# Fused block-sorted attention and maxout feed-forward on one core: zero blocks in front of item 0's scores and values, split last stores, and a new hand-written order

## The chip, the cores and the metric

The kernel runs on one core of one Trainium2 chip. The metric is the device time in microseconds (us) of one execution. The core has five instruction streams that run side by side and meet only at semaphores: TensorE (PE, with its weight loads shown as PEld), VectorE (DVE), ScalarE (ACT), GpSimd (POOL) and SyncE (SP). Each stream runs its own instructions strictly in the order in which they were issued.

## What is computed

```python
for _ in range(5):                       # sort_net: 4 items x 8 heads x 8 x 8
    P = np.exp(P - P.max(-1)); P = P / P.sum(-1); P = P / P.sum(-2)
k_sorted = einsum('bhij,bhjcd->bhicd', P, k_blocks)   # 8 blocks of 96 rows, 64 wide
v_sorted = einsum('bhij,bhjcd->bhicd', P, v_blocks)
scores = q_block @ k_sorted_block.T / 8               # each block against its own
attn = softmax(scores); x = attn @ v_sorted_block     # 3072 tokens x 512
g = maximum(x @ w1, x @ w2)                           # 512 -> 1024, twice
out = g @ w_out                                       # 1024 -> 512, float32
```

There are 4 items (the batch) of 768 tokens. Since `max(a, b) = relu(a - b) + b`, the kernel replaces w1 by w1 - w2, takes a relu, and adds `x @ (w2 @ w_out)` to the output. The output product itself is made by a Strassen-like scheme of seven products and a few sums.

## The kernel before

After a common start (the five normalisations, loads and first sorts) the whole rest is a list of short tokens, read from left to right by `token` (L917). The list is the order: each token issues its instructions on the engines at once, and every engine then runs its own share in that order. A final letter names the engine that empties PSUM (A is ScalarE, D is VectorE) or does the elementwise work (P is GpSimd). The first number is the item, mostly.

- `k`, `b`: sort a third of an item's keys (`sort_k`, L443) or a part of its values (L467 to L529) on TensorE, then cast them to SBUF. `q`: transposes of the queries. For items 0 and 1 TensorE makes them (L427); for items 2 and 3 the SP queue issues a DMA transpose (L417) from what `p` packed.
- `s b.u`: scores of unit u (`scores`, L533): eight matmuls, then one exponential on ScalarE (L551). `v b.u`: values of the same unit (`values`, L562): eight matmuls that need that exponential, then a reciprocal and a product on VectorE (L581, L587). `x b.t`: transposes of the result, on TensorE for item 0 (L608), as DMA transposes from the SP queue for the others (L600). x0.0 needs units 0 and 1, x0.1 units 2 and 3, x0.2 units 4 and 5, x0.3 units 6 and 7.
- `d`: w1 - w2 for a quarter of the columns. `T`: TensorE transposes of w2 (L633). `c`: the product w2 @ w_out (L652). `B`: the block diagonals of the later items' sorts (L319 to L337). `h`, or `ha` and `hb` for its halves: the first feed-forward product (L672) and its relu (L686, L688).
- `X`, `G`, `w`: sums for the Strassen-like product. `P i.n` and `U i.n`: its steps 0 to 6 (`Group.step`, L847; matmuls L800) for two tiles of 128 tokens and for one tile. Steps 5 and 6 each end in a store of the rows of one half of the tokens (L838 to L845), on the SP queue: 512 KB for P, 256 KB for U.
- `l`: loads, issued by GpSimd: `lk` keys, `lq` queries, `lv` and `lf` values. `y`: a small GpSimd copy that waits for the item's DMA transposes and so holds back what GpSimd issues after it. `t`: turns values on VectorE.

All PSUM results come from one ring of four buffers, taken in the order of the list (L63, L68). A token that needs a buffer waits until the result made four tiles earlier has been read. `keep_streaming` (L78) multiplies zeros into a PSUM tile that is written over afterwards. `scores` and `values` have an argument `n` for such zeros, and the list before never sets it:

```python
def scores(b, u, n=0):
    ...
    ps = ps_f32("s_ps")
    keep_streaming(ps, n)
```

Of the kernel before, what the change touches and what calls it, by code (L numbers as in the profile page):

```python
# [16 lines left out]
def kernel(  # L17
# [16 lines left out]
    nc = tc.nc  # L34
# [4 lines left out]
    B, H, S, D = q.shape  # L39
# [4 lines left out]
    DMODEL = H * D  # L44
# [9 lines left out]
    NW = DMODEL // 2  # L54
# [12 lines left out]
    def ps_f32(name):  # L67
        return psum.tile([128, 1024], FP32, tag="ps", name=name)  # L68
# [93 lines left out]
    def load_v(b, pieces=2, which=None, half=None):  # L162
        r0 = (b % 2 if half is None else half) * 64
        n = BLK * D // pieces
        for m in range(pieces) if which is None else [which]:
            nc.gpsimd.dma_start(  # L166
                out=v_raw[r0 : r0 + 64, m * n : (m + 1) * n],
                in_=v_src[b, :, m * n : (m + 1) * n],
            )
# [30 lines left out]
    def selections(b, eng=nc.gpsimd):  # L200
# [8 lines left out]
        if b == 0:  # L209
# [9 lines left out]
        out=one_j.rearrange("g (j x) -> g j x", x=130)[:, :, 0:128].rearrange(  # L219
            "g j (h w) -> g j h w", w=16  # L220
        )[:, :, :, 0:2],
        in_=ident[0:G, 0:8].to_broadcast([G, 8, 2, NB]).transpose([0, 3, 1, 2]),
# [548 lines left out]
    class Group:  # L771
# [63 lines left out]
                ins = nc.scalar.copy(out=out, in_=self.by_tile(self.bank(n)))  # L835
            return self.read(ins, n)

        def store(self, ch):  # L838
            tok0 = self.b * S + ch * TCH + self.tiles[0] * 128
            nc.sync.dma_start(  # L840
                out=out[tok0 : tok0 + len(self.tiles) * 128, :].rearrange(
                    "(t p) n -> p t n", p=128
                ),
                in_=self.o[ch],
            )  # L845

        def step(self, at, eng):  # L847
            a = self.by_tile(self.a) if at else None
            if at == 0:
                n = len(self.tiles)  # L850
                self.ps = ps_f32("out_ps")
                self.a = opool.tile([128, self.w], FP32, tag=f"a{n}", name="a", bufs=1)
                self.o = [
                    opool.tile([128, n, DMODEL], FP32, tag=f"o{n}", name="o", bufs=2)
                    for _ in range(2)
                ]
                self.product(0, "a11", "b11", True)
                self.first = self.copy(self.by_tile(self.a), 0, eng)
            elif at == 1:
                self.product(1, 2, 2, True)  # L860
                self.second = self.add(1, 0, 1, a, [self.first], eng)
            elif at == 2:
                self.product(0, "a12", "b21", False)
                self.copy(self.part(0, 0), 0, eng)
            elif at == 3:
                self.product(1, 1, 1, False)
                self.third = self.add(0, 1, 1, a, [self.first], eng)
            elif at == 4:
                self.product(0, 3, 3, True)
                self.fourth = self.add(1, 1, 0, self.part(0, 1), [self.third], eng)  # L870
            elif at == 5:
                self.product(1, 4, "b22", False)
                self.fifth = self.add(0, 1, 1, a, [self.first, self.fourth], eng)
                self.store(0)
            else:
                self.product(0, "a22", 4, False)
                self.add(
                    1, 0, 0, self.part(1, 0), [self.first, self.second, self.fifth], eng, True
                )
                self.store(1)  # L880

    first, second, both = slice(0, 64), slice(64, 128), slice(0, 128)
    keep_streaming(ps_f32("fill_ps"), 92 * 118, most=118)
# [8 lines left out]
    for c, n, m in [(2, 2, 0), (4, 3, 1)]:  # L892
        nc.gpsimd.tensor_copy(
            out=maskJ[:, c : c + n],
            in_=maskJ[:, m].to_broadcast([128, NB, n]).transpose([0, 2, 1]),
# [21 lines left out]
    def token(text):  # L917

        eng = text[-1] if text[-1].isalpha() else None
        body = text[:-1] if eng else text  # L920
        kind = body.rstrip("0123456789.")
        n = [int(x) for x in body[len(kind) :].split(".")]
        engine = {"P": nc.gpsimd, "D": nc.vector}.get(eng)
        if kind == "k":
            sort_k(*n, eng=eng)
        elif kind == "q":
            q_transposes(*n, eng)
        elif kind == "s":
            scores(*n)
        elif kind == "v":  # L930
            values(*n)
        elif kind == "x":
            x_transposes(*n, eng)
        elif kind == "t":
            turn_v(slice(0, 128), eng, n[1] * 24, n[1] * 24 + 24)
        elif kind == "b":
            {0: sort_v, 2: sort_v_pair, 3: sort_v_halved}[n[0]](*n, eng=eng)
        elif kind == "p":
            pair_q(*n, eng)
        elif kind == "y":  # L940
            nc.gpsimd.tensor_copy(
                out=landed.rearrange("p (c h n) -> p c h n", c=2, n=1),
                in_=xT[:, n[0] % 2, :, :, 0, 0:1],
            )
        elif kind == "lv":
            load_v(3, half=n[0])
        elif kind == "lk":
            load_k(n[0])
        elif kind == "lq":
            load_q(n[0])  # L950
        elif kind == "w":
            weight_sums(*n, engine)
        elif kind == "c":
            w_product(n[0], eng)
        elif kind == "X":
            x_sums(*n, engine)
        elif kind == "G":
            g_sums(*n, engine)
        elif kind == "h":
            moe_h(*n, eng=eng)  # L960
        elif kind == "ha":
            moe_h_products(*n, (0, 2))
        elif kind == "hb":
            moe_h(*n, eng, (1, 3))
        elif kind == "T":
            w2_transposes(n[0], eng)()
        elif kind == "d":
            w_difference(n[0], engine)
        elif kind == "B":
            block_diagonals([(0, 2), (0, 3), (1, 1), (1, 2), (1, 3)], 2)  # L970
        elif kind == "lf":
            load_v(1 + n[0] % 2, which=n[0] // 2)
        else:
            key = kind, n[0]
            if key not in groups:
                groups[key] = Group(n[0], (0, 1) if kind == "P" else (2,), n[0] > 0)
            groups[key].step(n[1], eng)

    groups = {}
    landed = const.tile([128, 4], BF16, tag="landed", name="landed")  # L980
    plan = [
        """
        d0P d1P k0.2D k0.1A b0.1D b0.2A b0.0A q0.0D b0.3A B0 q0.1D lk1 s0.4 s0.5 s0.0 v0.4 s0.7
        s0.6 v0.5 s0.3 v0.7 s0.1 v0.0 x0.2A v0.6 s0.2 v0.3 T0A v0.1 x0.3D T1D ha0.1.0 lq1 v0.2
        lf2 d3D ha0.1.1 lf3 x0.0D hb0.1.0A x0.1D hb0.1.1D w0.1D ha0.0.3 d2D ha0.1.3 hb0.1.3D
        G0.1.1D hb0.0.3A X0.3D ha0.1.2 ha0.0.1 hb0.0.1D hb0.1.2D G0.1.2D ha0.0.0 hb0.0.0A lf1
        lf0 G0.1.4D G0.0.1D X0.1D X0.2D w0.3D k1.1D k1.0A k1.2A c1D G0.1.3D c2D q1.0D q1.1A c0A
        s1.7 t1.3D s1.5 c3A G0.0.2D t1.2D G0.0.3D X0.4D s1.1 lq2 w0.2D s1.6 w1.1D s1.4 ha0.0.2
        t1.1D t1.0D hb0.0.2A s1.0 w1.2D P0.0D b2.2A G0.0.4D b2.0A w1.3D b2.1D P0.1D b2.6A b2.3A
        P0.2A b2.7D w1.4D b2.5A b2.4A p2.0A w0.4D P0.3D U0.0A v1.6 v1.7 x1.3 P0.4D U0.1D v1.4  # L990
        v1.5 U0.2A lk2 lk3 p2.1A x1.2 q2.0 P0.5D U0.3D v1.1 v1.0 lq3 P0.6D U0.4D k2.1D s1.2 s1.3
        U0.5D U0.6D x1.0 v1.2 q2.1 k2.0D k2.2A v1.3 h1.1.1A x1.1 X1.1D h1.1.2A s2.5 s2.1 h1.1.3A
        h1.1.0D G1.0.1D y1 s2.4 k3.0A k3.2A k3.1A lv1 h1.0.2A X1.2D v2.1 p3.0D G1.1.1D h1.0.1A
        v2.4 h1.0.0A s2.3 p3.1D G1.0.2D s2.6 q3.0 G1.1.2D h1.0.3A v2.5 G1.1.3D P1.0A G1.1.4D
        s2.0 s2.2 s2.7 X1.4D P1.1D q3.1 P1.2A X1.3D G1.0.3D lv0 v2.6 v2.7 P1.3D U1.0A x2.3
        G1.0.4D x2.2 v2.2 P1.4D U1.1D v2.3 t3.0D P1.5D P1.6D U1.2A v2.0 U1.3D U1.4D s3.3 x2.0
        x2.1 s3.0 t3.3D s3.6 t3.1D t3.2D U1.5D U1.6D h2.1.3D b3.2A X2.1D b3.3D h2.1.0A h2.1.1A
        X2.2D b3.0D b3.1A h2.0.1D s3.2 G2.1.1D s3.5 X2.3D G2.1.2D h2.1.2A v3.0 h2.0.3A X2.4D
        v3.3 v3.2 h2.0.0A G2.0.1D G2.0.2D h2.0.2A P2.0D G2.1.4D G2.0.4D G2.1.3D s3.1 s3.7 s3.4
        P2.1D v3.1 P2.2A U2.0D G2.0.3D x3.1 U2.1D v3.7 v3.6 P2.3D U2.2D v3.5 U2.3D v3.4 x3.3  # L1000
        x3.0 P2.4D U2.4D x3.2 P2.5D U2.5D U2.6D P2.6D h3.0.0D h3.1.3D h3.1.1D h3.0.1D X3.1D
        X3.3D h3.1.0D h3.1.2A G3.1.1D U3.0D G3.1.3D h3.0.3A h3.0.2A G3.1.2D P3.0A G3.0.1D
        G3.0.2D X3.2D G3.0.4D U3.1D P3.1D X3.4D U3.2A P3.2D U3.3D G3.1.4D G3.0.3D P3.3D P3.4D
        P3.5D U3.4D P3.6D U3.5D U3.6D
        """,
    ]
    for part in plan:
# [30 lines left out]
```

## Time and profile before

| quantity | value |
|---|---|
| three runs, median (lowest to highest) | 162.42 us (161.79 to 163.26) |
| the profiled execution, its own time | 162.45 us |
| span of its instructions | 160.7 us |
| mean granted clock of TensorE over the span | 0.985 |
| TensorE busy | 152.5 us, 95% |
| VectorE busy | 124.4 us, 77% |
| ScalarE busy | 77.0 us, 48% |
| GpSimd busy | 33.0 us, 21% |

A busy share is taken over the whole span, so it mixes stages that have different limits. "Granted clock" is the share of its full rate at which TensorE was allowed to run. A chain of waits lists what ended last, followed back from the last instruction. Times inside the profile count from the start of the span, and the execution's own time is 1.75 us longer than the span.

### The profile page before, as it was taken

Reading aid. Unit: us, or ns where it says so; the run is one execution under the profiler, and the core shown is the slowest. Engines: PE = TensorE matmul, PEld = TensorE weight load, DVE = VectorE, ACT = ScalarE, POOL = GpSimd, SP = SyncE. Lnnn points to the kernel's source line nnn. Section 1 sums busy time; section 2 is a strip of 40 time slices with the busy share of each in tenths; the row PEclk is TensorE's granted clock in tenths of the full one; section 3 lists DMA queues with packets and bytes.
Section 4 is the critical chain, followed back from the end, with each engine's and each line's share of the span. In section 5 each row is a group of like instructions: output and inputs, shape, how many; then the busy total and the mean of one; then the engine's idle time right before and its main releaser. Section 6 shows DMA issues by size and latency. Waiting matters only on the chain.

```text
span 160.7 us, 5090 instructions
## 1 busy us (share of the span) xinstructions
PE 152.5 (95%) x2224; PEld 117.6 (73%) x2224; DVE 124.4 (77%) x269; ACT 77.0 (48%) x98; POOL 33.0 (21%) x62
## 2 busy tenths in 40 slices
PE   7999899999999999999999999999999999999970
PEld 7938679666556889885767998766789985678850
DVE  4878887989996879993478798988788857975650
ACT  3587996224279994157878600576651000250000
POOL 7959998241230100000320000000000000000000
PEclk9999987999999999999999999999999999999998
DMA  3999999999999999699699983730100594000054
GB/s 38 205 205 198 182 189 205 210 205 214 220 201 204 211 173 158 131 367 126 133 164 197 165 165 131 234 135 0 35 18 0 115 250 177 0 4 0 0 209 185
DMA packets 30310, 23.93 MB, mean 149 GB/s; under 512 B 16784, under 2 KB 24976, under 8 KB 30288
## 3 DMA queue, kind: packets, MB, share of 16 engines
q0 software_dynamic: 11040, 13.37, 49.5%
q1 hardware_dynamic: 19248, 10.23, 26.5%
q8 instruction: 17, 0.28, 0.7%
q14 instruction: 5, 0.04, 0.1%
HBM read 26.75 MB, written 6.29 MB: 206 GB/s over the span
## 4 chain that ended last, share of the span: by engine, by line
PE 86%; DMA 5%; ACT 3%; POOL 2%; issue 1%; DVE 0%; POOLq 0%
PE out_ps L800 35%; PE h_ps L672 26%; DMA k_raw<-in_k_dram 5%; PE o_ps L570 5%; PE wc_ps L652 5%; PE k_ps L452 4%; PE s_ps L542 4%; ACT e L551 2%; PE tq_ps L427 2%; PE tw_ps L633 1%; PE v_ps L517 1%; PE v_ps L473 1%; PE tx_ps L608 1%; POOL v_raw L166 1%; PE v_ps L494 1%
## 5 line engine op out<-in xcount | busy, mean ns | idle before, releaser
L672 PE MATMUL h_ps<-xT,w_sb 128*128 128x384 bf16 x256 | 44.8, 326 | 0.1
L672 PEld LDWEIGHTS <-w_sb 128*128 128x128 bf16 x256 | 23.9, 98 | 14.7
L686 ACT ACTIVATE g<-h_ps 128x768 bf16<-128x768 f32 x20 | 16.3, 813 | 33.2 <-PE h_ps L672 33.2
L551 ACT ACTIVATE e<-s_ps 96x768 bf16<-96x768 f32 x32 | 23.8, 807 | 7.6 <-PE s_ps L542 7.5
L587 DVE TENSOR_TENSOR x<-o_ps,rs 96x512 bf16<-96x512 f32 x32 | 22.0, 687 | 1.1
L800 PEld LDWEIGHTS <-g 128*128 128x128 bf16 x192 | 18.4, 98 | 2.2
L826 DVE TENSOR_TENSOR o<-out_ps,a 128x512 f32<-128x512 f32 (+1 forms) x24 | 13.2, 554 | 4.3 <-PE out_ps L800 3.2
L688 DVE TENSOR_SCALAR g<-h_ps 128x768 bf16<-128x768 f32 x12 | 11.4, 955 | 6.3 <-PE h_ps L672 6.3
L800 PEld LDWEIGHTS <-sums_g 128*128 128x128 bf16 x144 | 13.8, 98 | 1.7
L800 PE MATMUL out_ps<-wo_sb,g 128*128 128x256 bf16 x96 | 13.1, 273 | 0.0
L570 PE MATMUL o_ps<-v_sb,e 96*128 96x65 bf16 x256 | 12.6, 197 | 0.2
L570 PEld LDWEIGHTS <-e 96*128 96x128 bf16 x256 | 11.2, 100 | 1.8 <-ACT e L551 0.5
L800 PE MATMUL out_ps<-w2T,sums_x 128*128 128x256 bf16 x72 | 11.8, 273 | 0.0
L826 DVE TENSOR_TENSOR o<-out_ps,o 128x512 f32<-128x512 f32 (+1 forms) x16 | 8.7, 553 | 3.5 <-PE out_ps L800 3.2
L109 ACT CAST v_sb<-v_ps 96x1024 bf16<-96x1024 f32 x11 | 10.6, 1013 | 1.5 <-PE v_ps L494 1.1
L542 PEld LDWEIGHTS <-kT 64*128 64x128 bf16 x256 | 6.3, 95 | 4.5 <-issue 3.3
L542 PE MATMUL s_ps<-qT,kT 64*128 64x96 bf16 x256 | 8.6, 206 | 1.0 <-DVE qT L111 0.5
L800 PEld LDWEIGHTS <-sums_x 128*128 128x128 bf16 x96 | 8.6, 97 | 1.1
L109 ACT CAST kT<-k_ps 128x1024 bf16<-128x1024 f32 x8 | 7.8, 1015 | 2.6 <-PE k_ps L452 2.6
L581 DVE RECIPROCAL rs<-o_ps 96x8 f32<-96x8 f32 x32 | 6.3, 198 | 3.2 <-PE o_ps L570 3.1
L157 POOL DMA_DIRECT2D k_raw<-in_k_dram x12 | 6.7, 564 | 8.3 <-DMA q_raw<-in_q_dram 3.8
L835 ACT COPY o<-out_ps 128x512 f32<-128x512 f32 (+1 forms) x6 | 2.9, 480 | 11.3 <-PE out_ps L800 11.3
(116 smaller groups left out, 243.5 us busy)
## 6 DMA issues: line engine op xcount, KB each, us to landing
out_dram<-o SPq DMA_DIRECT2D x8, 512.0 KB, 3.0
k_raw<-in_k_dram POOLq DMA_DIRECT2D x12, 256.0 KB, 11.9
v_raw<-in_v_dram POOLq DMA_DIRECT2D x8, 384.0 KB, 12.4
out_dram<-o SPq DMA_DIRECT2D x8, 256.0 KB, 3.0
w_sb<-in_moe_w_dram POOLq DMA_DIRECT2D x4, 256.0 KB, 6.1
w_sb<-in_moe_w_dram POOLq DMA_DIRECT2D x2, 512.0 KB, 9.4
wo_sb<-in_moe_w_out_dram POOLq DMA_DIRECT2D x2, 512.0 KB, 12.8
v_raw<-in_v_dram POOLq DMA_DIRECT2D x3, 256.0 KB, 4.9
```

Source lines behind the costliest of these rows:

```text
L109: nc.scalar.copy(out=out_ap, in_=in_ap)
L157: nc.gpsimd.dma_start(out=k_raw[b][:, ci * n : (ci + 1) * n], in_=k_src[b, :, ci * n : (ci + 1) * n],)
L542: nc.tensor.matmul(ps[:, h2 * 512 + ii * 128 : h2 * 512 + ii * 128 + BLK], kT[b][rows, (hp * 8 + i) * BLK : (hp * 8 + i) * BLK + 128], rhs ...
L551: nc.scalar.activation(out=e[:, 0 : 8 * BLK].rearrange("p (t c r) -> p t c r", t=8, r=R), in_=ps[0:BLK] .rearrange("p (t f) -> p t f", t=8 ...
L570: nc.tensor.matmul(ps[:, h2 * 512 + ii * 65 : h2 * 512 + (ii + 1) * 65], e[:, (h2 * 4 + ii) * BLK : (h2 * 4 + ii) * BLK + 128], v_sb[:, m0 ...
L587: nc.vector.tensor_tensor(out=x, in0=ov[:, :, :, 0:D], in1=rs.to_broadcast([BLK, 2, 4, D]), op=ALU.mult,)
L652: nc.tensor.matmul(ps[:, 0:512], w2T[:, fb, dmt * 128 : (dmt + 1) * 128], wo_sb[:, fb, :], start=(fb == 0), stop=(fb == NFB - 1),)
L672: nc.tensor.matmul(h_ps[ch, t][:, m * 512 : m * 512 + TCH], w1_sb[:, hp, fb * 128 : (fb + 1) * 128], xT[:, b % 2, ch, hp % 2, hp // 2, :], ...
L686: nc.scalar.activation(out=g, in_=src, func=AF.Relu)
L688: nc.vector.tensor_scalar(out=g, in0=src, scalar1=0.0, scalar2=None, op0=ALU.max)
L800: ins = nc.tensor.matmul(self.ps[:, bank * 512 + p * NW : bank * 512 + (p + 1) * NW], left(self.b, lw, k, ti * 128), right(rw, k), start=n ...
L826: ins = nc.vector.tensor_tensor(out=self.part(ch, half), in0=self.by_tile(self.bank(n)), in1=other, op=ALU.add)
```

## The change

`store` takes a range of columns and a queue. For the last item, the store of step 6 (512 columns) is cut into two: columns 256 to 511 are stored on the SP queue at step 4, when they are final, and columns 0 to 255 at step 6, issued by ScalarE. Tokens `F n` put n times 128 columns of zeros in front of the next `s` or `v`; there are six, 17 times 128 columns in all, around item 0's scores. The list has otherwise the same tokens in another order, and 36 of them have another engine letter.

```diff
-        def store(self, ch):
+        def store(self, ch, c0=0, c1=DMODEL, queue=nc.sync):
             tok0 = self.b * S + ch * TCH + self.tiles[0] * 128
-            nc.sync.dma_start(
-                out=out[tok0 : tok0 + len(self.tiles) * 128, :].rearrange(
+            queue.dma_start(
+                out=out[tok0 : tok0 + len(self.tiles) * 128, c0:c1].rearrange(
                     "(t p) n -> p t n", p=128
                 ),
-                in_=self.o[ch],
+                in_=self.o[ch][:, :, c0:c1],
             )
...
             elif at == 4:
                 self.product(0, 3, 3, True)
                 self.fourth = self.add(1, 1, 0, self.part(0, 1), [self.third], eng)
+                if self.b == B - 1:
+                    self.store(1, NW)
...
-                self.store(1)
+                if self.b < B - 1:
+                    self.store(1)
+                else:
+                    self.store(1, 0, NW, nc.scalar)
...
+        elif kind == "F":
+            fills[0] = n[0] * 128
         elif kind == "s":
-            scores(*n)
+            scores(*n, fills.pop(0, 0))
         elif kind == "v":
-            values(*n)
+            values(*n, fills.pop(0, 0))
...
-        d0P d1P k0.2D k0.1A b0.1D b0.2A b0.0A q0.0D b0.3A B0 q0.1D lk1 s0.4 s0.5 s0.0 v0.4 s0.7
-        s0.6 v0.5 s0.3 v0.7 s0.1 v0.0 x0.2A v0.6 s0.2 v0.3 T0A v0.1 x0.3D T1D ha0.1.0 lq1 v0.2
-        lf2 d3D ha0.1.1 lf3 x0.0D hb0.1.0A x0.1D hb0.1.1D w0.1D ha0.0.3 d2D ha0.1.3 hb0.1.3D
-        G0.1.1D hb0.0.3A X0.3D ha0.1.2 ha0.0.1 hb0.0.1D hb0.1.2D G0.1.2D ha0.0.0 hb0.0.0A lf1
-        lf0 G0.1.4D G0.0.1D X0.1D X0.2D w0.3D k1.1D k1.0A k1.2A c1D G0.1.3D c2D q1.0D q1.1A c0A
-        s1.7 t1.3D s1.5 c3A G0.0.2D t1.2D G0.0.3D X0.4D s1.1 lq2 w0.2D s1.6 w1.1D s1.4 ha0.0.2
...
-        v1.5 U0.2A lk2 lk3 p2.1A x1.2 q2.0 P0.5D U0.3D v1.1 v1.0 lq3 P0.6D U0.4D k2.1D s1.2 s1.3
-        U0.5D U0.6D x1.0 v1.2 q2.1 k2.0D k2.2A v1.3 h1.1.1A x1.1 X1.1D h1.1.2A s2.5 s2.1 h1.1.3A
-        h1.1.0D G1.0.1D y1 s2.4 k3.0A k3.2A k3.1A lv1 h1.0.2A X1.2D v2.1 p3.0D G1.1.1D h1.0.1A
-        v2.4 h1.0.0A s2.3 p3.1D G1.0.2D s2.6 q3.0 G1.1.2D h1.0.3A v2.5 G1.1.3D P1.0A G1.1.4D
...
-        G3.0.2D X3.2D G3.0.4D U3.1D P3.1D X3.4D U3.2A P3.2D U3.3D G3.1.4D G3.0.3D P3.3D P3.4D
-        P3.5D U3.4D P3.6D U3.5D U3.6D
+        k0.2A k0.1D b0.1A b0.3A q0.0D lk1 b0.0D d0P b0.2A F2 s0.1 q0.1D F3 s0.4 d1P F4 v0.1 s0.2 F2 v0.4
+        s0.0 s0.3 F4 v0.2 lq1 v0.0 s0.7 v0.3 s0.6 F2 s0.5 x0.0D v0.7 x0.1A v0.5 ha0.0.0 hb0.0.0A v0.6
+        x0.2A lf2 T1A d2D x0.3D X0.1D lf3 T0D ha0.0.1 hb0.0.1D ha0.1.0 hb0.1.0A ha0.0.2 ha0.1.1
+        d3D hb0.0.2D B0 ha0.1.2 hb0.1.2D hb0.1.1D ha0.0.3 ha0.1.3 G0.0.1D w0.1D lf1 lf0 X0.3D
+        hb0.0.3A hb0.1.3D X0.2D k1.1A c3A G0.0.2D G0.1.1D w0.3D c0A G0.1.3D k1.0A k1.2A G0.0.4D
+        q1.0D G0.1.2D G0.1.4D q1.1A G0.0.3D c1D X0.4D s1.6 t1.2D s1.5 t1.3D s1.0 t1.0D s1.4 c2A
...
+        lk3 v1.4 x1.2 v1.6 x1.3 P0.6D U0.2A v1.0 U0.3D lq3 U0.4D s1.3 s1.2 v1.1 U0.5D v1.3 p2.1A
+        U0.6D k2.2A x1.0 k3.0D v1.2 h1.1.1D h1.1.2D x1.1 k2.0A q2.0 k3.1D k2.1A X1.1D y1 lv1
+        k3.2D h1.1.0A h1.1.3D q2.1 h1.0.1D h1.0.2D G1.1.1D G1.0.1D s2.5 lv0 s2.4 h1.0.0A G1.1.2D
+        X1.2D s2.3 s2.2 h1.0.3A G1.1.3D G1.0.2D v2.5 G1.1.4D P1.0A v2.3 P1.1D p3.0D v2.4 G1.0.4D
...
+        X3.3D h3.1.1D h3.0.0D G3.1.1D h3.0.1D G3.0.2D h3.0.3D P3.0D G3.1.2D h3.0.2A G3.1.3D
+        P3.1D G3.0.3D U3.0A G3.1.4D P3.2A G3.0.4D P3.3D U3.1D X3.4D P3.4D U3.2D P3.5D P3.6D
+        U3.3D U3.4D U3.5D U3.6D
```

More of the change, by code (lines that the diff above doesn't have):

```diff
@@ L977, in token @@
             groups[key].step(n[1], eng)
-    groups = {}
+    groups, fills = {}, {}
     landed = const.tile([128, 4], BF16, tag="landed", name="landed")
@@ L989 @@
-        t1.1D t1.0D hb0.0.2A s1.0 w1.2D P0.0D b2.2A G0.0.4D b2.0A w1.3D b2.1D P0.1D b2.6A b2.3A
-        P0.2A b2.7D w1.4D b2.5A b2.4A p2.0A w0.4D P0.3D U0.0A v1.6 v1.7 x1.3 P0.4D U0.1D v1.4
-        v1.5 U0.2A lk2 lk3 p2.1A x1.2 q2.0 P0.5D U0.3D v1.1 v1.0 lq3 P0.6D U0.4D k2.1D s1.2 s1.3
-        U0.5D U0.6D x1.0 v1.2 q2.1 k2.0D k2.2A v1.3 h1.1.1A x1.1 X1.1D h1.1.2A s2.5 s2.1 h1.1.3A
-        h1.1.0D G1.0.1D y1 s2.4 k3.0A k3.2A k3.1A lv1 h1.0.2A X1.2D v2.1 p3.0D G1.1.1D h1.0.1A
-        v2.4 h1.0.0A s2.3 p3.1D G1.0.2D s2.6 q3.0 G1.1.2D h1.0.3A v2.5 G1.1.3D P1.0A G1.1.4D
@@ L995 @@
[L995 to L1000, printed above, removed]
@@ L1001 @@
-        x3.0 P2.4D U2.4D x3.2 P2.5D U2.5D U2.6D P2.6D h3.0.0D h3.1.3D h3.1.1D h3.0.1D X3.1D
-        X3.3D h3.1.0D h3.1.2A G3.1.1D U3.0D G3.1.3D h3.0.3A h3.0.2A G3.1.2D P3.0A G3.0.1D
-        G3.0.2D X3.2D G3.0.4D U3.1D P3.1D X3.4D U3.2A P3.2D U3.3D G3.1.4D G3.0.3D P3.3D P3.4D
-        P3.5D U3.4D P3.6D U3.5D U3.6D
+        k0.2A k0.1D b0.1A b0.3A q0.0D lk1 b0.0D d0P b0.2A F2 s0.1 q0.1D F3 s0.4 d1P F4 v0.1 s0.2 F2 v0.4
+        s0.0 s0.3 F4 v0.2 lq1 v0.0 s0.7 v0.3 s0.6 F2 s0.5 x0.0D v0.7 x0.1A v0.5 ha0.0.0 hb0.0.0A v0.6
@@ new lines @@
+        x0.2A lf2 T1A d2D x0.3D X0.1D lf3 T0D ha0.0.1 hb0.0.1D ha0.1.0 hb0.1.0A ha0.0.2 ha0.1.1
+        d3D hb0.0.2D B0 ha0.1.2 hb0.1.2D hb0.1.1D ha0.0.3 ha0.1.3 G0.0.1D w0.1D lf1 lf0 X0.3D
+        hb0.0.3A hb0.1.3D X0.2D k1.1A c3A G0.0.2D G0.1.1D w0.3D c0A G0.1.3D k1.0A k1.2A G0.0.4D
+        q1.0D G0.1.2D G0.1.4D q1.1A G0.0.3D c1D X0.4D s1.6 t1.2D s1.5 t1.3D s1.0 t1.0D s1.4 c2A
+        t1.1D w0.2D w1.1D lq2 s1.7 s1.1 w1.2D w1.3D lk2 P0.0D b2.0A b2.2A b2.1D P0.1D b2.3A
+        b2.6A P0.2A b2.7D w1.4D b2.5A b2.4A P0.3D w0.4D P0.4D p2.0A U0.0A v1.5 v1.7 P0.5D U0.1D
@@ new lines @@
+        lk3 v1.4 x1.2 v1.6 x1.3 P0.6D U0.2A v1.0 U0.3D lq3 U0.4D s1.3 s1.2 v1.1 U0.5D v1.3 p2.1A
+        U0.6D k2.2A x1.0 k3.0D v1.2 h1.1.1D h1.1.2D x1.1 k2.0A q2.0 k3.1D k2.1A X1.1D y1 lv1
+        k3.2D h1.1.0A h1.1.3D q2.1 h1.0.1D h1.0.2D G1.1.1D G1.0.1D s2.5 lv0 s2.4 h1.0.0A G1.1.2D
+        X1.2D s2.3 s2.2 h1.0.3A G1.1.3D G1.0.2D v2.5 G1.1.4D P1.0A v2.3 P1.1D p3.0D v2.4 G1.0.4D
+        p3.1A s2.7 X1.4D X1.3D s2.1 P1.2A U1.0A q3.0 G1.0.3D s2.6 s2.0 U1.1D U1.2A q3.1 v2.7
+        U1.3D U1.4D v2.0 v2.6 P1.3D x2.2 x2.3 U1.5D U1.6D v2.1 x2.0 v2.2 P1.4D s3.0 x2.1 t3.3D
@@ new lines @@
+        s3.1 P1.5D s3.5 t3.2D t3.0D s3.2 t3.1D s3.3 P1.6D h2.1.0A h2.1.2D b3.3D G2.0.1D b3.2A
+        h2.1.3A b3.1A X2.1D b3.0D h2.0.0A h2.0.2A v3.3 v3.0 h2.1.1A X2.2D v3.1 G2.1.1D X2.3D
+        h2.0.1A G2.0.3D h2.0.3A v3.2 P2.0A s3.4 s3.6 G2.0.2D G2.1.2D X2.4D s3.7 G2.0.4D P2.1D
+        v3.5 P2.2D U2.0A v3.7 v3.6 G2.1.3D x3.0 U2.1D G2.1.4D U2.2A x3.3 P2.3D v3.4 x3.2 U2.3D
+        U2.4D P2.4D U2.5D x3.1 U2.6D P2.5D P2.6D h3.1.2D h3.1.0D G3.0.1D X3.1D X3.2D h3.1.3A
+        X3.3D h3.1.1D h3.0.0D G3.1.1D h3.0.1D G3.0.2D h3.0.3D P3.0D G3.1.2D h3.0.2A G3.1.3D
```

## The prediction

> **What bounds the kernel now.** I read the granted clock first, then the chain of waits in order of time, then the stretch and the end that the change touches. In the chain, three columns: start, length, what.
>
> ```profile
> 17.04 0.25 PE pe L319 x5
> ...
> 18.40 3.63 ACT e L551 x5
> ...
> 22.07 0.35 PE s_ps L542 x8
> ...
> 30.50 0.34 PE tx_ps L608 x8
> 30.84 7.15 PE h_ps L672 x44
> ...
> 142.40 13.11 PE out_ps L800 x120
> ...
> 155.54 0.42 DVE o L826
> ```
>
> TensorE carries the chain from 22.07 to 155.51 almost alone (one piece on ScalarE, at 48.8). Before that, for 3.63 us, item 0's exponentials on ScalarE carry it. So a gain can come from three places: the exponentials' stretch, TensorE's own speed, and the end. The next view cuts the early part into stretches of 2 us (stretch, its length, busy time of PE, PEld, DVE, ACT, POOL, then the granted clock).
>
> ```profile
> 18.00:20.00 2.00, 1.32 (x36) 1.02 (x33) 1.97 (x8) 1.69 (x4) 2.00 (x4) 1.00 1.36 181
> 20.00:22.00 2.00, 1.61 (x40) 1.31 (x40) 1.75 (x6) 2.00 (x4) 1.84 (x1) 1.00 1.25 176
> 22.00:24.00 2.00, 1.93 (x34) 1.67 (x35) 1.68 (x5) 1.81 (x4) 1.77 (x1) 0.65 1.23 203
> 24.00:26.00 2.00, 2.00 (x29) 1.86 (x29) 1.78 (x4) 1.21 (x2) 2.00 (x5) 0.50 1.24 204
> 26.00:28.00 2.00, 2.00 (x41) 1.91 (x40) 1.24 (x3) 1.52 (x1) 1.38 (x2) 0.99 1.23 205
> ```
>
> TensorE stands idle for 1.07 of 4 us (18 to 22), and then its clock is at half from about 22.6 to 26.0. After 26 it is 1.00 to the end of the work. Half a clock over 3.4 us, with TensorE busy, costs up to 1.7 us. The end, as the timeline has it (start, length, engine, and in brackets the idle time before):
>
> ```profile
> 152.98 3.99 SPq L840 DMA_DIRECT2D out_dram<-o  x4
> ...
> 155.54 0.42 DVE L826 TENSOR_TENSOR o<-out_ps,o 128x256 f32<-128x256 f32 x1 [0.23 <-PE out_ps L800]
> ```
>
> The last sum ends at 155.96, but the last store starts only at 156.6 (the last start among L840's issues), because SP still issues the one before; it was 1.05 us long, the slowest of 16 whose median is 0.38. From 155.96 to the end of the span there are 4.7 us. Last, the four DMA transposes of packed queries, from issue to landing:
>
> ```profile
> DMA to landing us min/median/max: 5.3/6.8/8.7
> ```
>
> **The change, part by part.** All sums stand against the profiled execution, 162.45 us (span 160.7 and 1.75 around it), which is 0.03 above the median.
>
> *The zeros.* 17 times 128 columns. A matmul of 256 columns follows the next after 0.109 us (12 of L800 in 1.31), one of 512 after 0.23 (8 of L652 in 1.83 to 1.85), so six blocks cost about 0.95 us of TensorE time. They lie in waits for exponentials. In the old order 1.07 us were idle there; if that cover were gone they would cost their 0.95.
>
> *Item 0's stretch.* In the new order ScalarE does one key cast (k0.2) right behind k0.0's, and then the three casts of values that before ended at 18.08. The old second key cast started at 14.21, the new one can start when k0.0's ends, at 13.65. The three took 2.83, so the exponentials can begin at about 17.7, not 18.40. Seven of them took 5.03 before, so eight take 5.75; with 0.7 for places where ScalarE waits for scores the last ends at 24.15. Behind it on TensorE come v0.5 0.24, eight h matmuls 1.30, v0.6 0.24, two x at 0.34 and two w2 transposes at 0.90 (the full-clock row): 4.26, to 28.4. At 30.84 the old order stood four h matmuls further (0.65) and had B done (0.25 at 17.04, and 0.2 for two more changes of matrix shape). So 28.4 + 0.65 + 0.45 = 29.5 against 30.84: a gain of 1.3. Ends: 2.0 with no waits for scores, 0.65 if the exponentials start at 18.4 again.
>
> That gain needs the full clock. Between the first score and the last exponential, 6.1 to 6.8 us, TensorE now has 8 scores (0.28), 7 values (0.24), one q transpose (0.80), two x (0.34) and the zeros (0.95): 6.4 us, so it is filled, where before 1.07 of 4 us were empty. If the clock still halves for one 3.4 us stretch, 1.45 is lost (1.7 less a part that falls into waits). I take the full clock, since the stretches before 18, with TensorE busy 0.82 of the time or more, kept it.
>
> The Trainium skill speaks against this. "TensorE: Matmul & The Clock Gate", section "Why this matters for your kernels", asks only that no idle gap be longer than about 3 us. Here no gap between 18 and 22.6 is longer than 0.46 us, and the clock fell all the same, so the trace disagrees; by the page the zeros would change nothing, and the sum would be that of the clock rival below.
>
> *B and the GpSimd order.* B's VectorE work (about 1.8 us, between 17.4 and 19.2) moves behind item 0's first h products. GpSimd now issues item 1's key loads (1.67 us) before the two w1 - w2 products of 2.17 and 2.12; the first of these ends near 23.5, before the h matmuls at 24.4. Cover 0.9 us, cost nothing; without the cover 1.7.
>
> *VectorE between 28 and 48.* It was busy 3.96 and 3.98 of 4 us from 40 to 48. The new order puts c1's cast behind a q copy (0.96) and three G sums (0.55 each), and the fourth score after it (s1.4) needs c1's PSUM buffer. Cover is the three scores before it, 0.5 us. Cost 0 to 1.0; I take 0.2, since one key cast (1.22), one c cast (0.68) and one x copy (0.54) have left VectorE for 0.95 of relu and B's 1.8.
>
> *Changes of matrix shape.* Eight h matmuls take 1.41 behind scores and 1.30 otherwise, so a change costs 0.1. Counted in the program's order from the first h on there are 41 against 40: 0.1.
>
> *Item 2's queries.* q2.0 and q2.1 were apart, one before x1.0 and one before x1.1; now both follow x1.1 on SP. From the end of v1.2, x1.1's issue can start after k3.0's cast and v1.2's two VectorE steps, at +2.0, takes 1.3, so q2.0 is issued at +3.3. Six h tokens (1.30) and four key thirds (0.55 with shape changes: 96 took 1.64) lie before s2.5: it is due at +10.0. Landings of 5.3, 6.8, 8.7 give +8.6, +10.1, +12.0: a wait of 0, 0.1 or 2.0. q2.1 follows 1.4 to 2.2 later and is due at +11.8 (s2.3): nearly the same. I take 0.3. Queued behind s2.5 on TensorE is everything else. x1.2 to x1.0 no longer stand behind q2.0. Items 2 and 3 otherwise: the same tokens, no wait that I can place.
>
> *The end.* ScalarE is free there, so the last store starts 0.1 after the last sum: 0.55 earlier. It is half as large: 128 KB at the 400 GB/s moved between 156 and 158, 0.3. P's last store, half a MB before, is now halved and four U steps ahead of the end, so less is queued in front: 0.15. Gain 1.0. A store on ScalarE's queue is not in the trace: ends 1.2, and a loss of 1.6 if it landed after 5.1 (the slowest of L840) rather than 3.0 (its median); the nearest row is the last SP store, and it is what I took.
>
> Sum: -1.3 + 0.2 + 0.1 + 0.3 - 1.0 = -1.7, so 162.45 becomes 160.75; I write 160.7.
>
> **The rivals.**
> *The clock falls all the same* (or in another stretch: the half-clock stretch may begin anywhere). For it: the sum above fills the stretch but leaves four or five short waits for exponentials. Against it: less than half of the old idle time is left. Then -1.3 becomes +0.15, and the time is 162.2.
> *Slower: item 2's queries come late.* One mechanism: four DMA transposes back to back on SP, with GpSimd's value loads (lv1) released beside them, since y1 waits for x1.1 alone. With the slowest rows (issue of an x 2.12, of a q 3.65, landing 8.7) q2.0 is issued at +4.1 and lands at +12.8, a wait of 2.8; q2.1 is issued at +7.8 and lands at +16.5, due at 14.6, 1.9 more. 4.7 for 0.3 gives 165.1. It decides from 2.0 us of wait on. Against it: those slowest rows are the pair at 84 to 95, beside four value loads, and now the loads start about 3 us behind q2.0.
> *The end gains nothing* because the first store on ScalarE's queue costs as much as the slowest SP issue (1.05): 161.7.
>
> **How the numbers follow.** Forecast 0.58, clock 0.20, queries 0.12, end 0.10. The forecast's own range is 159.3 to 161.8 (stage 0.65 to 2.0, end 0.5 to 1.2). One per cent of 162.42 is 1.62, about what a measurement of this kernel can tell from no change: below 160.80 is faster, above 164.04 slower. Of the forecast 0.35 lies below 160.80, and 0.03 of the other cases. Slower has 0.08 of the queries' case and 0.06 from the clock's with a lost end or a late query. The range 159.4 to 163.3 leaves out the best tenth and the queries' case.
>
> **What would show it.** Granted clock 1.00 from 18 to 30: if a 0.5 is left, the zeros failed. The first exponential near 17.7 and the w2 transposes done near 28.4. No idle time at s1.4 (near 47). Idle time in front of s2.5's weight loads that a DMA ends is the slow rival. From the last sum to the end of the span 3.7 us, not 4.7. The prediction is wrong if TensorE shows other idle time after 30.

## The result and the profile after

The changed kernel takes 172.88 us (median of 4 runs, 170.43 to 173.16), beside 162.1 for the kernel before on the same chip: a ratio of 1.062, with a 95% interval of 1.054 to 1.070. The ratio counts only fast runs, those within 1.5% of the fastest run of their kernel (two of the four here, 170.43 and 172.76), so it is not the quotient of the two medians. The profiled execution took 172.99 us, its span is 170.9, and TensorE's mean granted clock over it is 0.970. It is slower by 10.2 us of span, where 1.7 less was forecast.

The chain of waits of the changed kernel, in order of time (start, length, what), shows the place:

```profile
75.03 0.36 SPq L417
75.39 0.05 issue
75.44 16.15 DMA qT<-q_pair
91.59 0.04 issue
91.63 0.82 PE s_ps L542 x16
```

The chain no longer lies on TensorE from 22 us on: for 16.15 us it lies on one DMA transpose, q2.1. The instructions that touch the queries qT, between 70 and 95 us, give the landings that answer to the line of before (5.3/6.8/8.7 for the four transposes):

```profile
L417 SPq DMA_TRANSPOSE qT<-q_pair x2: 1600/1711/1822, 73.8 to 75.4; - x2
...
  DMA qT<-q_pair: 9.0, 1
...
DMA to landing us min/median/max: 5.5/10.8/16.1
```

q2.0 was issued at 73.79 and landed in 5.55, in time for s2.5 and s2.4. q2.1 was issued 1.65 us later and took three times as long. The second line is what s2.3 waited, on TensorE's stream, with the whole rest of the kernel queued behind it. Beside q2.1 GpSimd issued item 2's four value loads (lv1 and lv0), from 76.14 to 77.68, the first 0.70 us behind q2.1. They too were late: they landed after 15.1 to 18.4 us, where the same four had taken 4.8 to 9.6.

The stretches of 2 us, for the part around item 0's exponentials as before, and for the wait (busy time of PE, PEld, DVE, ACT, POOL, then the granted clock, the DMA share and GB/s):

```profile
18.00:20.00 2.00, 2.00 (x47) 1.42 (x41) 1.58 (x4) 1.84 (x4) 2.00 (x4) 1.00 1.37 177
20.00:22.00 2.00, 1.99 (x47) 1.32 (x42) 1.76 (x5) 1.98 (x3) 1.94 (x4) 1.00 1.24 164
22.00:24.00 2.00, 1.80 (x43) 1.39 (x41) 1.93 (x6) 1.93 (x3) 2.00 (x2) 1.00 1.21 199
24.00:26.00 2.00, 2.00 (x30) 1.41 (x27) 1.93 (x5) 1.18 (x2) 2.00 (x2) 1.00 1.24 205
26.00:28.00 2.00, 2.00 (x44) 1.94 (x43) 1.63 (x4) 1.73 (x3) 1.27 (x3) 1.00 1.24 206
...
84.00:86.00 2.00, 0.00 (x0) 0.00 (x0) 0.54 (x2) 0.00 (x0) 0.00 (x0) 1.00 1.00 61
86.00:88.00 2.00, 0.00 (x0) 0.00 (x0) 0.00 (x0) 0.00 (x0) 0.00 (x0) 0.54 1.59 83
88.00:90.00 2.00, 0.00 (x0) 0.00 (x0) 0.00 (x0) 0.00 (x0) 0.00 (x0) 0.50 0.64 119
90.00:92.00 2.00, 0.37 (x10) 0.37 (x12) 0.00 (x0) 0.00 (x0) 0.00 (x0) 0.50 1.04 209
```

In the early part the granted clock is 1.00 throughout and only 0.21 of TensorE's 6 us from 18 to 24 are idle (the zeros count as busy): in this execution that part did what was meant. From 84.5 to 91.6 all five streams stand, and up to 90 the DMA engines move 61 to 119 GB/s, less than the 164 to 206 of the rows above. The clock falls during the wait: it is at half from 86.17 to 96.41.

The end, from the timeline of the changed kernel:

```profile
161.19 5.28 SPq L840 DMA_DIRECT2D out_dram<-o  x4
...
164.42 2.73 ACTq L840 DMA_DIRECT2D out_dram<-o  x2
...
166.34 0.42 DVE L826 TENSOR_TENSOR o<-out_ps,o 128x256 f32<-128x256 f32 x1 [0.23 <-PE out_ps L800]
```

The last sum ends at 166.76 and the last store is issued by ScalarE at 166.79, without the 0.6 us that it waited for SP before. From there to the end of the span it takes 4.1 us instead of 4.7.

The account of the 10.2 us: +9.0 wait; +2.4 for the 4.78 us (91.63 to 96.41) in which TensorE then worked at half its clock (half of that time, an estimate); -0.8 in item 0's stretch (the w2 transposes end at 28.95, and with the prediction's 1.1 for work that had moved, 30.05 stands against 30.84); -0.6 at the end; the rest, +0.2, is spread.

### The profile page after: what moved, and what is told of

Same layout as the page of the kernel before. It is cut to its first block, busy times and chain, and to the rows that moved or that the text cites. A ratio compares the mean times of both kernels' runs of the same rounds, so it can differ in the third digit from the quotient of the medians.

```text
span 170.9 us, 5102 instructions
## 1 busy us (share of the span) xinstructions
PE 154.2 (90%) x2227; PEld 117.2 (69%) x2230; DVE 126.9 (74%) x269; ACT 77.5 (45%) x98; POOL 32.7 (19%) x62
## 4 chain that ended last, share of the span: by engine, by line
PE 78%; DMA 14%; POOL 2%; ACT 2%; issue 1%; DVE 0%; SPq 0%; ACTq 0%; POOLq 0%
PE out_ps L800 33%; PE h_ps L672 22%; DMA qT<-q_pair 9%; DMA k_raw<-in_k_dram 5%; PE o_ps L570 5%; PE wc_ps L652 4%; PE s_ps L542 4%; PE k_ps L452 3%; PE tq_ps L427 2%; PE v_ps L517 1%; PE v_ps L473 1%; PE tw_ps L633 1%; ACT e L551 1%; PE tx_ps L608 1%; POOL v_raw L166 1%
## 5 line engine op out<-in xcount | busy, mean ns | idle before, releaser
L672 PE MATMUL h_ps<-xT,w_sb 128*128 128x384 bf16 x256 | 45.3, 332 | 0.0
L672 PEld LDWEIGHTS <-w_sb 128*128 128x128 bf16 x256 | 24.6, 99 | 15.9 <-issue 1.0
L686 ACT ACTIVATE g<-h_ps 128x768 bf16<-128x768 f32 x15 | 12.2, 811 | 33.4 <-PE h_ps L672 33.4
L688 DVE TENSOR_SCALAR g<-h_ps 128x768 bf16<-128x768 f32 x17 | 16.1, 954 | 5.3 <-PE h_ps L672 5.3
L542 PE MATMUL s_ps<-qT,kT 64*128 64x96 bf16 x256 | 9.1, 209 | 9.2 <-DMA qT<-q_pair 9.0
L800 PE MATMUL out_ps<-w2T,sums_x 128*128 128x256 bf16 x72 | 11.8, 273 | 0.0
L800 PE MATMUL out_ps<-wc,xT 128*128 128x256 bf16 x48 | 8.3, 285 | 0.0
```

The costliest lines, as they stand in the source:

```text
L542: nc.tensor.matmul(ps[:, h2 * 512 + ii * 128 : h2 * 512 + ii * 128 + BLK], kT[b][rows, (hp * 8 + i) * BLK : (hp * 8 + i) * BLK + 128], rhs ...
L672: nc.tensor.matmul(h_ps[ch, t][:, m * 512 : m * 512 + TCH], w1_sb[:, hp, fb * 128 : (fb + 1) * 128], xT[:, b % 2, ch, hp % 2, hp // 2, :], ...
L686: nc.scalar.activation(out=g, in_=src, func=AF.Relu)
L688: nc.vector.tensor_scalar(out=g, in0=src, scalar1=0.0, scalar2=None, op0=ALU.max)
L800: ins = nc.tensor.matmul(self.ps[:, bank * 512 + p * NW : bank * 512 + (p + 1) * NW], left(self.b, lw, k, ti * 128), right(rw, k), start=n ...
```

## The experiments

Two theories stood at the start. *Collision*: q2.1 and the value loads, started within a microsecond of each other, slow each other down; each is harmless alone. *Row of four*: four DMA transposes close together on the SP queue are slow by themselves. Each run has its own runs of the kernel before beside it, and ratios are to these. The diffs show only the part of the list that changes, joined over line ends. Times inside a kernel are those of its one profiled execution.

**1. Hold the loads until q2.1 is in** (`e1_guard`). `y1` also reads a column of what q2.0 and q2.1 write, and the token stands behind q2.1.

```diff
             nc.gpsimd.tensor_copy(
                 out=landed.rearrange("p (c h n) -> p c h n", c=2, n=1),
                 in_=xT[:, n[0] % 2, :, :, 0, 0:1],
             )
+            nc.gpsimd.tensor_copy(
+                out=landed[:, 0:2].rearrange("p (h n) -> p h n", n=1),
+                in_=qT[2][:, 0::2, 0, 0:1],
+            )
...
-        x1.1 k2.0A q2.0 k3.1D k2.1A X1.1D y1 lv1 k3.2D h1.1.0A h1.1.3D q2.1 h1.0.1D
+        x1.1 k2.0A q2.0 k3.1D k2.1A X1.1D k3.2D h1.1.0A h1.1.3D q2.1 y1 lv1 h1.0.1D
```

> The changed kernel, but GpSimd's y step also reads one column of both halves of item 2's transposed queries and stands behind q2.1 in the list, so that the four value loads (lv1, lv0) are issued only when q2.1 has landed. Theory 'collision' (q2.1 and the four value loads, in flight together, slow each other): q2.1 lands 5 to 8 us after its issue instead of 16.15, TensorE waits under 1 us in front of s2.3 instead of 9.0, the clock stays at 1.00 there, and the time is 161 to 162 us. Rival 'row of four' (four DMA transposes that follow each other on SP are slow by themselves, whatever GpSimd loads): q2.1 still takes about 16 us, time near 172.

Measured: 161.24 us, ratio 0.997 (0.993 to 1.000). The waits of this kernel between 70 and 100 us (who waited for what: total, times, longest):

```profile
POOL landed L948 <- DMA xT<-x: 20.1, 1, 20.1
...
POOL landed L952 <- DMA qT<-q_pair: 5.4, 1, 5.4
```

GpSimd now waits for q2.1, which costs nothing, and TensorE does not wait for it. The two transposes take 5.65 and 5.33 us, though they are as close together on SP as before, and the loads, issued from 81.7, take 4.7 to 10.0. The whole loss is gone: the row of four is not the cause.

What the two do to each other is seen in the traffic by DMA queue: packets, MB, and the time of the packets as a share of 16 engines (it can exceed 100%, as packets of one engine overlap in time or reach beyond the window). q1 carries the transposes and SP's other DMAs, q0 what GpSimd issues. First the changed kernel, from 80 to 84 us, with both in flight:

```profile
q0 software_dynamic: 37, 0.19, 80.2%
q1 hardware_dynamic: 232, 0.06, 27.9%
```

Then this experiment, from 75.7 to 81.1 us, while its two transposes were in flight alone:

```profile
q1 hardware_dynamic: 2919, 0.73, 105.9%
```

and from 84 to 87 us, the loads alone:

```profile
q0 software_dynamic: 111, 0.58, 102.9%
```

Per microsecond, the transposes move 541 packets alone (2919 in 5.4 us) and 58 beside the loads; the loads move 37 packets alone (0.19 MB) and 9 (0.05 MB) beside the transposes. The packets of a transpose are small (0.25 KB), those of a load 5 KB. In these stretches the two do not share the engines' rate: both fall, one to a ninth and the other to a quarter. The Trainium skill, "DMA: Bandwidth & Descriptors", section "Queues, rings and completion order", has each DMA engine take turns between queues, a whole packet at a time (there a group of descriptors, which need not be one packet of the profile); both rows moving at once agrees with that, but it does not give the fall of the sum. The same page's "Rules for kernel authors" says "A transpose next to ordinary DMAs needs nothing". That row is about wrong data; read as a statement on time it would be off by the 9 us of this wait.

**2. Put the two transposes back in their old places** (`e2_oldplace`), q2.0 before x1.0 and q2.1 before x1.1, in the new list.

```diff
-        U0.6D k2.2A x1.0 k3.0D v1.2 h1.1.1D h1.1.2D x1.1 k2.0A q2.0 k3.1D
+        U0.6D q2.0 k2.2A x1.0 q2.1 k3.0D v1.2 h1.1.1D h1.1.2D x1.1 k2.0A k3.1D
-        h1.1.3D q2.1 h1.0.1D
+        h1.1.3D h1.0.1D
```

> The changed kernel with q2.0 and q2.1 put back between the x transposes (q2.0 in front of x1.0, q2.1 between x1.0 and x1.1), y1 and the loads unchanged: since y1 waits for x1.1, which is behind q2.1 on SP, the loads start after q2.1 again. Both theories expect a fast kernel: 160.5 to 162 us, q2.1 landing in 5 to 7 us. If it stays near 172, neither is right and the cause lies elsewhere in the new list.

Measured: 165.01 us, ratio 1.022 (1.015 to 1.030): a miss. The collision is gone (the loads start at 81.6, and q2.1 lands at 80.40), but its waits from 60 to 100 us show another:

```profile
PEld L672 <- issue: 3.0, 1, 3.0
PE h_ps L672 <- DMA xT<-x: 2.7, 1, 2.7
```

x1.1 now stands behind q2.1 on SP and is issued at 76.39 (72.46 in the changed kernel), and the new list has put the h products that read it earlier. The profile names x1.1 for 2.7 of the 3.3 us lost. So the new list needs x1.1 in front of q2.1, which is what brings q2.1 beside the loads that x1.1 releases.

**3. Move only q2.1 behind x1.1 in the old list** (`e3_before_q`).

```diff
-        U0.5D U0.6D x1.0 v1.2 q2.1 k2.0D k2.2A v1.3 h1.1.1A x1.1 X1.1D
+        U0.5D U0.6D x1.0 v1.2 k2.0D k2.2A v1.3 h1.1.1A x1.1 q2.1 X1.1D
```

> The kernel before with one token moved: q2.1 from between x1.0 and x1.1 to behind x1.1, so that y1 no longer covers it and the four value loads start beside it. 'Collision': q2.1 lands 12 to 17 us after its issue, TensorE waits 4 to 9 us in front of s2.3 (due near 84), the clock halves behind it, 167 to 172 us. 'Row of four': only x1.0, x1.1 and q2.1 follow each other, as two x and a q do elsewhere, so 162 to 163.5 us.

Measured: 161.81 us, ratio 1.002 (0.998 to 1.006): a miss for the collision as I had put it, that is, for any overlap. Here q2.1 was issued at 73.46 and the first load at 76.91, 3.45 us later, and q2.1 landed after 4.74, at 78.20. Counted from issue to landing, the two overlap for 1.3 us without harm. But no packets of the two met. From 77 to 78 us only q1 moves any:

```profile
q1 hardware_dynamic: 485, 0.12, 63.2%
```

and from 78 to 79 only q0:

```profile
q0 software_dynamic: 15, 0.09, 94.8%
```

The first load's first packet came about 1.2 us behind its issue, when the transpose's were through. So it matters how much of the transpose is left when the loads begin to move. Runs 5, 6, 7 and 11 bear on that.

**4. Run 1 without the zeros** (`e4_nofill`): all six `F` tokens are taken out of the list.

```diff
-        b0.2A F2 s0.1 q0.1D F3 s0.4 d1P F4 v0.1 s0.2 F2 v0.4 s0.0 s0.3 F4 v0.2 lq1 v0.0 s0.7 v0.3 s0.6 F2 s0.5
+        b0.2A s0.1 q0.1D s0.4 d1P v0.1 s0.2 v0.4 s0.0 s0.3 v0.2 lq1 v0.0 s0.7 v0.3 s0.6 s0.5
```

> The kernel e1 without the six blocks of zeros. If the zeros hold the clock: a stretch of 3.4 us at half clock between 20 and 28, and 0.8 to 1.5 us more than e1. If the new order alone fills the stretch: the clock stays 1.00 and the time is that of e1, within 0.4.

Measured: 160.86 us, ratio 0.994 (0.990 to 0.997). The mean granted clock is 0.993 or more in all 10 runs, and in the profile it is 1.00 up to 158.94. In the new order the zeros are not needed for the clock. Without them the w2 transposes end at 28.55, with them at 28.48 in run 1 and at 28.95 in the changed kernel; the two ratios (0.994, 0.997) have overlapping intervals. So no cost of the zeros is seen here.

**5. Two loads beside q2.1, two held back** (`e5_two`): lv0 waits behind a token `z` that reads what q2.1 writes.

```diff
-        s2.5 lv0 s2.4
+        s2.5 z0 lv0 s2.4
```

> The changed kernel with two of the four value loads (lv1) where they were, beside q2.1, and the other two (lv0) held until q2.1 has landed. 'Collision', with a harm that grows with what is loaded beside it: q2.1 lands 9 to 13 us after its issue, a wait of 2 to 6 us in front of s2.3, 164 to 169 us. If the harm is all or nothing: 16 us and 172 as in the changed kernel, or 5 to 6 us and 161 as in e1.

Measured: 167.93 us, ratio 1.036 (1.027 to 1.045). q2.1 landed after 11.30 us instead of 16.15, TensorE waited 5.0 for it, and the two loads took 8.2 and 9.8. These two loads also started 0.8 us earlier against q2.1, which left more of the transpose to be met, and the harm was smaller all the same. It grows with what is loaded.

**6. Start the loads later** (`e6_delay`), by four dummy GpSimd memsets (2.26 us) behind `y1`, everything else as in the changed kernel.

```diff
                 in_=xT[:, n[0] % 2, :, :, 0, 0:1],
             )
+            for _ in range(4):
+                nc.gpsimd.memset(one_j.bitcast(U32), 0)
```

> The changed kernel with about 2.5 us of GpSimd work (four memsets of a finished tile) between y1 and the four loads, which then start 3.2 us behind q2.1's issue instead of 0.7, about as in e3. All four loads still run beside the end of q2.1. If the harm needs the loads' first data to meet a transpose that is not yet moving: q2.1 lands in 5 to 7 us, 161 to 162 us. If it is a matter of the share of the DMA engines alone: 8 to 13 us, 163 to 169.

Measured: 161.32 us, ratio 0.996 (0.992 to 1.001). The first load is issued 2.14 us behind q2.1, still 3.2 us before that lands. q2.1 takes 5.32 us, the loads 5.6 to 9.5. Here, too, the packets hardly met. From 80 to 80.8 us only q1 moves any:

```profile
q1 hardware_dynamic: 908, 0.23, 127.4%
```

and from 80.85 to 82 only q0:

```profile
q0 software_dynamic: 31, 0.19, 81.5%
```

In the 0.05 us between, the last 43 packets of the transpose moved beside the first 16 of the loads. So the overlap that both cases of the expectation assume did not occur, and run 6 cannot tell them apart.

**7. The collision in the kernel before** (`e7_early_loads`): `y1` there waits for what x1.1 reads instead of what it writes, so the loads start about 6 us earlier, at 73.1. Nothing else of the change is in it.

```diff
+        turned[b, t] = x
...
-                out=landed.rearrange("p (c h n) -> p c h n", c=2, n=1),
-                in_=xT[:, n[0] % 2, :, :, 0, 0:1],
+                out=landed[0:BLK, 0:2].rearrange("p (h n) -> p h n", n=1),
+                in_=turned[n[0], 1][:, 0, 0, :, 0:1],
```

> The kernel before with one wait changed: y1 waits for what x1.1 reads instead of what it writes, so the four value loads start about 4 us earlier, beside q2.1 and x1.1 in their old places. 'Collision': q2.1 or x1.1 lands 10 to 18 us after its issue, TensorE waits 4 to 12 us for it and the clock halves behind the wait, 167 to 176 us. If something else in the new list is needed for the harm: 162 to 164.

Measured: 171.41 us, ratio 1.059 (1.051 to 1.068), nearly the loss of the changed kernel without any of its change. Here the transpose that TensorE waits for is x1.1, issued 1.08 us behind the first load, and it took 12.39 us to land (4.05 in the kernel before). When the first load packet moved, at 76.76, some 860 packets of q2.1 and x1.1 were left; q2.1, issued 1.52 us before the first load, took 7.7. The timeline of TensorE in this kernel (in brackets the idle time before, and what ended it):

```profile
78.73 0.50 PE L673 MATMUL h_ps<-xT,w_sb 128*128 128x384 bf16 x2
86.63 2.08 PE L673 MATMUL h_ps<-xT,w_sb 128*128 128x384 bf16 x6 [7.40 <-DMA xT<-x]
```

**8. The split stores alone** (`e8_before_stores`): the kernel before with the `store` part of the change and its old list.

> The kernel before with the split last stores alone. The prediction's term: 1.0 us less (0.5 to 1.2), 160.7 against 161.7. By the changed kernel's profile, where the end took 4.1 us behind the last sum instead of 4.7: 0.6 less. Rival (a first store on ScalarE's queue costs what it saves): within 0.2.

Measured: 160.64 us, ratio 0.990 (0.984 to 0.996). Its end, in the timeline:

```profile
150.39 4.04 SPq L840 DMA_DIRECT2D out_dram<-o  x4
...
153.67 1.40 ACTq L840 DMA_DIRECT2D out_dram<-o  x2
154.26 0.42 DVE L826 TENSOR_TENSOR o<-out_ps,o 128x256 f32<-128x256 f32 x1 [0.23 <-PE out_ps L800]
```

The last store is issued at 154.72, 0.04 after the last sum, and lands after 2.32; from the sum to the end of the span it is 3.5 us.

**9. The zeros alone** (`e9_zeros`): the same 17 times 128 columns in the old list, in the stretch where its TensorE waited.

```diff
-        s0.4 s0.5 s0.0 v0.4 s0.7 s0.6 v0.5 s0.3 v0.7 s0.1
+        s0.4 s0.5 s0.0 F4 v0.4 F3 s0.7 s0.6 F4 v0.5 F2 s0.3 F2 v0.7 F2 s0.1
```

> The kernel before, its old list, with the same 17 times 128 columns of zeros in six blocks in front of item 0's scores and values, where its TensorE waited between 18 and 22.6 us; nothing else. If the zeros keep the clock up, no execution has a half-clock stretch in the middle: the mean clock stays at 0.991 or more in every run (in 42 runs of the kernel before, some 19 lie at 0.978 to 0.987), and the ratio is 0.993 to 0.998. If zeros do nothing for the clock, runs at 0.985 or less appear as often as before and the ratio is 1.00 to 1.006, the zeros costing up to their 0.95 us where the cover is short.

Measured: 161.65 us, ratio 0.999 (0.996 to 1.002); the mean clock is 0.992 or more in all 12 runs, and below 0.986 in 6 of the 23 of the kernel before beside them. (In the 42 runs that the expectation counts, 18 lie at 0.978 to 0.987, not 19.) Half of the expectation came true: no execution lost its clock, but no gain in time is clear of the noise. The stretches of 2 us in this kernel:

```profile
20.00:22.00 2.00, 1.99 (x45) 1.42 (x44) 1.52 (x4) 1.83 (x4) 1.76 (x1) 1.00 1.31 177
22.00:24.00 2.00, 1.91 (x45) 1.50 (x45) 1.90 (x7) 2.00 (x4) 1.42 (x2) 1.00 1.23 206
```

**10. The new order alone** (`e10_order`): run 4 with the old last stores.

> The new list with the value loads held until both query transposes of item 2 are in, without the zeros and with the old last stores: the new order alone. By the prediction's sum (item 0's stretch -1.3, the rest +0.6) it is 0.7 us faster than before, ratio 0.9955. If the split stores are worth 1.0 us or more by themselves (the run with them alone gave 0.990), and the new list with them gave 0.9937, then the new order is worth nothing: ratio 0.998 to 1.004. The clock should be full (0.993 or more) in every run, as it was with the stores split.

Measured: 161.54 us, ratio 1.000 (0.997 to 1.002): the second case. The order, with its collision removed, is worth nothing that these runs can tell from zero.

**11. Half the delay of run 6** (`e11_delay2`): two memsets in place of four.

> The changed kernel with two dummy GpSimd memsets (about 1.1 us) in front of item 2's value loads, so that the first load is issued about 1.0 to 1.5 us behind q2.1, between 0.7 us (which gave a landing of 16 us and 172.9) and 2.1 us (5.3 us and 161.3). If the harm goes with how far the transpose has got when the loads begin, q2.1 takes 6 to 12 us and the time lies between, 162 to 168. If it is all or nothing, the time is either 161 or 172.

Measured: the profiled execution took 165.6 us, the only other one 160.72. In the profiled one the first load came 1.00 us behind q2.1, q2.1 landed after 8.42, and TensorE waited 2.1 for it. When the first load packet moved, at 81.11, only 56 packets of the transpose were left, yet 33 of them waited until after 81.5, the last until 84.3, among the loads' packets (81.5 to 85 us):

```profile
q0 software_dynamic: 157, 0.77, 108.7%
q1 hardware_dynamic: 33, 0.00, 1.3%
```

So a small rest of the transpose is enough to hold up its landing, and near this point the kernel came out either way in its two executions.

Together (the distance is from q2.1's issue to the first load's; the packets are those that q2.0 and q2.1 still had to move when the first load packet moved, of some 2900 for both):

| run | first load behind q2.1 | loads | packets left | q2.1's landing | ratio of the kernel |
|---|---|---|---|---|---|
| changed kernel | 0.70 us | 4 | some 820 | 16.15 us | 1.062 |
| 5 | -0.10 | 2 | some 1580 | 11.30 | 1.036 |
| 11 | 1.00 | 4 | 56 | 8.42 | two runs, 165.6 and 160.7 us |
| 6 | 2.14 | 4 | 43, through in 0.05 us | 5.32 | 0.996 |
| 3 | 3.45 | 4 | 0 | 4.74 | 1.002 |
| 1 | 6.01 | 4 | 0 | 5.33 | 0.997 |

The shorter the distance, the more is left, and where much is left the harm is large (run 5 has more left, but two loads in the way and not four). Where the transposes' packets were through, or gone within 0.05 us, neither side was slowed.

Runs 4 and 8 beat the changed kernel, and by 0.6% and 1.0% the kernel before (both intervals lie below 1); their intervals overlap, and the smaller edit of the two is 8.

## Why the prediction was wrong

**Item 2's queries: the step that failed.** The text has for q2.1 "due at +11.8 (s2.3): nearly the same", and 0.3 us for both; the wait was 9.04. The first half held: q2.0 landed in 5.55 us, between the rows' 5.3 and 6.8, and s2.5 did not wait. For q2.1 the lowest, median and highest of four landings of the kernel before were used, and in none of the four did loads join a transpose whose packets were moving. The slowest (8.7) was issued 3.6 to 5.2 us after loads that were already under way, and no packet of a transpose moved from 84.5 to 88 us: it waited for the loads, but they were not mixed.

The mechanism itself was named, as the slower rival: transposes "with GpSimd's value loads (lv1) released beside them, since y1 waits for x1.1 alone". Two of its terms were wrong. Its argument against, that "the loads start about 3 us behind q2.0", measured from the wrong transpose: the loads started 2.35 us behind q2.0, but 0.70 us behind q2.1, and run 6 shows that 1.4 us more would have been enough. And its price, 4.7 us, came from the slowest rows, which were taken as the worst that can happen; the wait was twice that. The half clock behind it, 2.4 us more, was not counted in this rival: 9 us of idle time were paid for as 11.4. Half-clock stretches came with the other waits of this kind too (10.24 us with the 7.40 of run 7, 3.41 with the 5.0 of run 5 and the 2.1 of run 11), but not with the 2.7 of run 2's profile.

**Item 0's stretch** (-1.3) held as a milestone in part: the exponentials began at 17.95 (17.7 forecast), the w2 transposes were done at 28.95 (28.4 forecast; 28.48 in run 1), a gain of 0.8. But the gain was counted against one execution of the kernel before that had lost its clock between 22.6 and 26.0, and this is not what that kernel always does: in 65 runs beside these experiments the mean clock is at 0.986 or less in 24, with a median of 162.17 us, and at 0.991 or more in 41, with a median of 161.29. So the lost clock costs 0.9 us, in about a third of the runs. In an execution of the old list with its clock (run 8's) the h products that follow start at 29.40, against 30.68 in the profile before, 1.28 sooner. With 30.84 less 1.28, 29.56, the new order's 28.55 + 1.1 = 29.65 in run 4 (29.58 by run 1) is no gain. Run 10 says the same of the whole time.

**The zeros** (cost 0, covered). In the old list no execution lost its clock with them (run 9), but the time did not fall clearly below that of the kernel before, whose runs include those without its clock. The 17 of its 23 runs beside them that kept the clock have a mean of 161.32 us, the 12 runs with the zeros 161.52: whether the zeros cost these 0.2 us is not shown, as single runs scatter by 0.4. In the new list they are not needed (run 4). The doubt about the rule on idle gaps, raised in the prediction, stands: with no gap above 0.46 us from 18 to 22.6 the clock fell in the profile before, and with the same longest gap it stayed at 1.00 in run 8's.

**The end** (-1.0): right within what the runs can tell. Run 8 gives 1.6 us by its ratio (0.7 to 2.5 by its interval), 1.2 by the means of the executions that kept their clock at 0.991 or more (160.1 in three, 161.2 in seven), and 1.2 by the profile (3.5 us from the last sum to the end, for 4.7); in the changed kernel's profile it is 0.6. A store on ScalarE's queue landed after 2.2 to 2.9 us in runs 4 and 8 and in the changed kernel, so the rival that it gains nothing has fallen.

**VectorE between 28 and 48**, **B and the GpSimd order**: s1.4 waited 0.16 us for c1's cast (0.2 taken), and TensorE waited 0.22 for w1 - w2 in run 10, where 0 was taken. **Changes of matrix shape** were not tried by themselves.

**What was to show it.** "Idle time in front of s2.5's weight loads that a DMA ends" was the right place but for the unit: it stood in front of s2.3.

What is not settled: why the packets of a transpose and of loads slow each other so much when both are left to move. The packet counts show that they do, and that the harmless runs are those in which they did not meet; they do not show what inside the DMA engines does it. And the repeat runs show that the clock is lost in some executions of the kernel before, not what decides which.

## What to carry to other kernels

Where a change lets a DMA transpose and a group of loads start within a microsecond of each other, price the transpose at three times its usual landing (16.15 us for 5.3 and 12.39 for 4.05 here), not at the slowest row of a trace in which they never met; and look at the distance to each transpose, the last one above all. Whether two transfers met is seen in the packets of each queue, not in the times from issue to landing. Here a semaphore wait on an idle engine, or 2 us of delay for the loads, removed the whole loss, so when a reordering costs far more than its parts, look first at what it made simultaneous. A gain that consists of getting back a lost clock should be counted only in the share of runs that lose it, and that share is not in one profile.

## What the hardware did that was not expected

- A transpose that takes 5.3 us alone took 16.15 with four loads beginning 0.70 us behind it, and the loads 15.1 to 18.4 instead of 4.8 to 9.6; issued 2.14 us behind it, they moved their first packet as the transpose's last ones went (80.80 to 80.85 us), and neither was slowed.
- Half-clock stretches come in whole units: 3.41 us in the kernel before and in run 11, 10.24 (three of them) from within the 9.04 us wait on, and full-clock stretches of 150.19 and 153.60 (44 and 45 of them) in runs 1 and 4. The Trainium skill, "TensorE: Matmul & The Clock Gate", section "What's actually happening", gives a window of 3413 ns that runs freely; these lengths agree. That its phase against the kernel decides whether the clock is lost would fit with the third of the runs, but no run here varied it.
